# Decode attention with grouped queries on one core: scores with queries in rows, probabilities transposed back, values two chunks at once

## The chip, the cores and the metric

The kernel runs on one core of one Trainium2 chip. Its time is the device time of one execution in microseconds (us), and the median of the runs is quoted. Each kernel was run in three or five rounds beside the kernel before on the same chip, and every profile quoted is of a run that counts as fast: at most 1.5% above the fastest run of the same kernel in its call. Medians are of all runs. A ratio is the mean time of one kernel's fast runs over that of the other's of the same rounds, so it is not quite the ratio of the medians that stand beside it. A profile is taken of one execution; its span is the time from the first to the last instruction, 1.7 to 1.9 us less than the time of that execution in nearly all runs.

## The reference

Eight sequences of four new tokens attend to a cache of 2048 keys and values with 8 K/V heads of 128; each K/V head serves four query heads. All inputs are bf16.

```python
B, Sq, D = 8, 4, 512
Hq, Hkv, Sk, Dh = 32, 8, 2048, 128
q = (x @ wq).reshape(B, Sq, Hq, Dh).transpose(0, 2, 1, 3)
k = jnp.repeat(k_cache, rep, axis=1)          # rep = 4
v = jnp.repeat(v_cache, rep, axis=1)
scores = jnp.einsum("bhqd,bhkd->bhqk", q, k) * Dh ** -0.5
p = softmax(scores)
o = jnp.einsum("bhqk,bhkd->bhqd", p, v)
out = o.transpose(0, 2, 1, 3).reshape(B, Sq, Hq * Dh) @ wo
```

K and V are 67 MB together, the weights 8 MB more. Each byte is used for 16 queries only, so the kernel is a race between loading the cache and touching it once.

## The kernel before

The work is cut into 32 units: a pair of K/V heads of one sequence, with 1 MB of K and 1 MB of V. A unit has 32 chunks of keys, 64 keys of each head in the 128 partitions. K is transposed on TensorE (two bf16 read as one fp32), copied to SBUF, and used as the stationary operand of the scores, with the 32 query columns moving. The exps write probabilities with keys in the partitions, which is the layout in which they then move against V as the stationary operand. The sums of the softmax are a matmul with a matrix of ones. Transposes run 3.5 units ahead of the values.

```python
pad0 = const.tile([128, 192], BF16, name="pad0")     # first of the const tiles
...
ones = const.tile([128, 128], BF16, name="ones")
pad = const.tile([128, 64], BF16, name="pad")        # read and written by nothing
probs = [const.tile([128, C, NQ], BF16, name=f"probs{i}") for i in range(L // 2 + 2)]
...
def scores(i):                                        # a half unit
    for j in range(HC // 2):
        for e in range(2):
            nc.tensor.matmul(s_ps[:, 2*j : 2*j+2, :], lhsT=k_t[:, j % (HC // 4), :, e],
                             rhs=q_bd[:, p, e, b, :, :], start=(e == 0), stop=(e == 1))
    for g in range(2):                                # exp straight into probs
        nc.scalar.activation(out=pr[rows, ..., cols], in_=s_ps[rows, :, cols], func=EXP)

def values(i):
    for c in range(HC):
        nc.tensor.matmul(o_ps[u][:, :], lhsT=vs[u][:, cc, :], rhs=pr[:, cc, :], ...)

def norms(u):                                         # ones x probs, reduce, reciprocal
    ...
def finish(u):                                        # one multiply, o_ps * r_sb -> oT
    ...
for step in range(-L - 1, NH):                        # NH = 64 half units
    ...                                               # transposes, scores, transposes
    if step >= 0:
        if hf == 0:
            norms(u)
        values(step)
        if hf == 1:
            finish(u)
    load_ready(...)                                   # K: 7 buffers, V: 6
...
to_tokens(2)                                          # end: oT -> rows of wo, projection
project(1, 0, 4); to_wo_rows(2); project(1, 4, 4); ...
```

The softmax here doesn't subtract the row's maximum and nothing guards it: scores larger than these inputs give would overflow.

## Time and profile before

| | before |
|---|---|
| median of the runs | 189.3 us at first, 189.4 to 189.8 in later rounds |
| the execution that was profiled first | 192.02 us, span 190.2, mean clock 0.972 |
| bytes moved | 75.97 MB, mean 399 GB/s |
| busy: TensorE / VectorE / ScalarE | 83% / 59% / 45% |
| chain that ended last | DMA 97% |

The chain is read from the end back: for each piece of work, what released it. Where it says DMA for 97%, the time is that of the loads. Busy shares say less; TensorE at 83% is idle whenever it waits for K. The lines themselves stand in the prediction.

### The profile page before, as it was taken

What the parts mean: (1) busy time and instruction counts of PE and PEld (TensorE: products, weight loads), DVE (VectorE), ACT (ScalarE), POOL (GpSimd) and SP (SyncE); (2) the same over time, 40 slices, a digit from 0 to 9 for tenths busy, and PEclk for the clock granted to TensorE, in tenths of its full rate; (3) what the DMA queues carried; (4) which work ended last, traced back from release to release, by engine and by line L of the source; (5) the groups of instructions that cost most, each with busy time, mean ns of one, the idle gap of its engine ahead of it and who ended that gap; (6) DMA issues with size and microseconds to landing.
All of it is one profiled execution on the core that took longest, in us unless ns stands there. A gap on an engine that the chain in (4) does not pass through costs nothing.

```text
span 190.2 us, 6461 instructions
## 1 busy us (share of the span) xinstructions
PE 156.9 (83%) x2899; PEld 139.3 (73%) x2899; DVE 113.0 (59%) x218; ACT 86.4 (45%) x170; POOL 6.3 (3%) x9
## 2 busy tenths in 40 slices
PE   0536596999978888999988999978888889999693
PEld 0516396899967777889977888878877778886471
DVE  0580545577756666757766666665666668676420
ACT  2003656565555555445555555554555554454000
POOL 8400000000000000000000000000000000000000
PEclk9999879999999999999999999999999999999858
DMA  6999999999999999999999999999999999999970
GB/s 245 451 407 382 383 394 394 386 385 387 397 419 426 422 426 424 426 422 427 424 424 426 426 422 431 417 427 422 426 424 427 420 429 420 424 424 415 416 310 22
DMA packets 10955, 75.97 MB, mean 399 GB/s; under 512 B 1288, under 2 KB 1416, under 8 KB 2568
## 3 DMA queue, kind: packets, MB, share of 16 engines
q1 hardware_dynamic: 10880, 75.55, 96.4%
q8 instruction: 22, 0.36, 0.7%
q14 instruction: 5, 0.04, 0.1%
q10 hardware_dynamic: 48, 0.02, 0.0%
HBM read 75.53 MB, written 0.03 MB: 397 GB/s over the span
## 4 chain that ended last, share of the span: by engine, by line
DMA 97%; SPq 1%; issue 0%; PE 0%; ACT 0%
DMA k_sb<-in_k_cache_dram 69%; DMA v_sb<-in_v_cache_dram 8%; DMA wo_e<-in_wo_dram 8%; DMA wq_sb<-in_wq_dram 7%; DMA wo_sb<-in_wo_dram 4%; SPq L131 0%; PE out_ps L376 0%; SPq L111 0%; ACT out_sb L430 0%; SPq L121 0%
## 5 line engine op out<-in xcount | busy, mean ns | idle before, releaser
L195 PE MATMUL kp<-ident,k_sb 128*128 128x128 f32 x512 | 82.7, 288 | 20.5 <-DMA k_sb<-in_k_cache_dram 10.5
L202 DVE COPY kt<-kp 128x1024 bf16<-128x1024 bf16 x96 | 65.5, 686 | 28.3 <-PE kp L195 27.4
L266 ACT ACTIVATE probs<-s_ps 64x256 bf16<-64x256 f32 x128 | 48.5, 379 | 69.9 <-PE s_ps L256 69.1
L195 PEld LDWEIGHTS kp<-ident,k_sb 128*128 128x128 f32 x512 | 55.8, 144 | 23.9 <-DMA k_sb<-in_k_cache_dram 12.5
L256 PE MATMUL s_ps<-q_bd,kt 128*128 128x64 bf16 x1024 | 42.5, 195 | 3.1 <-ACT kt L200 1.9
L256 PEld LDWEIGHTS <-kt 128*128 128x128 bf16 x1024 | 40.0, 99 | 5.5 <-ACT kt L200 2.2
L280 PEld LDWEIGHTS <-v_sb 128*128 128x128 bf16 x1024 | 34.4, 96 | 9.5 <-DMA v_sb<-in_v_cache_dram 2.1
L200 ACT COPY kt<-kp 128x1024 bf16<-128x1024 bf16 x32 | 32.4, 1012 | 12.6 <-PE kp L195 11.8
L280 PE MATMUL o_ps<-probs,v_sb 128*128 128x32 bf16 x1024 | 35.1, 177 | 1.2 <-DMA v_sb<-in_v_cache_dram 1.1
L302 DVE TENSOR_REDUCE l_sb<-l_ps 128x32 f32<-128x512 f32 x32 | 22.1, 692 | 21.2 <-PE l_ps L294 21.2
L294 PE MATMUL l_ps<-probs,ones 128*128 128x512 bf16 x64 | 19.0, 379 | 0.0
L306 DVE RECIPROCAL r_sb<-l_sb 128x32 f32<-128x32 f32 x32 | 11.3, 353 | 1.1
L311 DVE TENSOR_TENSOR oT<-o_ps,r_sb 128x32 bf16<-128x32 f32 x32 | 5.8, 182 | 1.9 <-PE o_ps L280 1.7
L294 PEld LDWEIGHTS <-ones 128*128 128x128 bf16 x64 | 6.1, 98 | 0.5
L430 ACT CAST out_sb<-out_ps 64x256 bf16<-64x256 f32 x1 | 0.4, 366 | 13.1 <-PE out_ps L376 13.1
L376 PE MATMUL out_ps<-wo_sb,oP 128*32 128x256 bf16 x48 | 5.5, 393 | 0.1
L171 POOL MEMSET wo_e<- 64x6144 bf16 x1 | 5.2, 5212 | 0.3 <-POOLq L447 0.3
L243 DVE CAST q_bd<-pse 64x512 bf16<-64x512 f32 x4 | 2.6, 683 | 4.3 <-PE pse L234 4.3
L376 PEld LDWEIGHTS <-oP 128*32 128x32 bf16 x48 | 3.5, 137 | 1.4 <-issue 0.2
L178 DVE COPY pick<-ident 128x64 bf16<-128x64 bf16 x4 | 0.6, 220 | 6.5 <-POOL ident masks.py:199 6.5
L219 PE MATMUL psq<-xT_sb,wq_sb 128*128 128x32 bf16 x128 | 3.5, 186 | 0.3 <-DVE xT_sb L213 0.3
L219 PEld LDWEIGHTS <-wq_sb 128*128 128x128 bf16 x128 | 3.5, 103 | 0.3 <-issue 0.3
(41 smaller groups left out, 31.9 us busy)
## 6 DMA issues: line engine op xcount, KB each, us to landing
k_sb<-in_k_cache_dram SPq DMA_DIRECT2D x32, 1024.0 KB, 19.6
v_sb<-in_v_cache_dram SPq DMA_DIRECT2D x32, 1024.0 KB, 19.4
wq_sb<-in_wq_dram SPq DMA_DIRECT2D x1, 4096.0 KB, 14.1
wo_sb<-in_wo_dram SPq DMA_DIRECT2D x4, 512.0 KB, 14.8
wo_sb<-in_wo_dram SPq DMA_DIRECT2D x4, 256.0 KB, 9.6
wo_m<-in_wo_dram SPq DMA_DIRECT2D x1, 512.0 KB
wo_e<-in_wo_dram SPq DMA_DIRECT2D x8, 60.0 KB
x_sb<-in_x_dram SPq DMA_DIRECT2D x1, 32.0 KB
```

What stands on the lines that cost most here:

```text
L195: nc.tensor.transpose(kp[:, j, :], k4[:, w : w + 128], ident4[:, :])
L200: nc.scalar.copy(out=kt2, in_=kp2)
L202: nc.vector.tensor_copy(out=kt2, in_=kp2)
L219: nc.tensor.matmul(psq[:, h, :], lhsT=wq_sb[:, r, hh * 128 : (hh + 1) * 128], rhs=xT_sb[:, r, :], start=(r == 0), stop=(r == R - 1),)
L256: nc.tensor.matmul(s_ps[:, 2 * j : 2 * j + 2, :], lhsT=k_t[:, j % (HC // 4), :, e], rhs=q_bd[:, p, e, b, :, :], start=(e == 0), stop=(e == 1),
L266: nc.scalar.activation(out=pr[rows, hf * HC : (hf + 1) * HC, cols], in_=s_ps[rows, :, cols], func=EXP)
L280: nc.tensor.matmul(o_ps[u][:, :], lhsT=vs[u][:, cc, :], rhs=pr[:, cc, :], start=(cc == 0), stop=(cc == C - 1),)
L294: nc.tensor.matmul(l_ps[:, :, :], lhsT=ones[:, :], rhs=pr[:, c : c + LC, :], start=(c == 0), stop=(c + LC == C),)
L302: nc.vector.tensor_reduce(out=l_sb[:, :], in_=l_ps[:, :, :].rearrange("d c q -> d q c"), axis=AX, op=ADD)
L306: nc.vector.reciprocal(r_sb[:, :], l_sb[:, :])
L311: nc.vector.tensor_tensor(out=oT[(p + 1) // 2][:, :, (p == 2) * 1, b, :], in0=o_ps[u][:, :].rearrange("d (h s) -> d h s", h=HP), in1=r_sbs ...
L376: nc.tensor.matmul(out_ps[half * T : (half + 1) * T, :], lhsT=o, rhs=w[:, half * DH : (half + 1) * DH], start=(p == 0 and r == 0), stop=(p ...
```

## The change

The intent is to take work off TensorE and ScalarE. The scores use the small query matrix as the stationary operand (32 columns, four column tiles at once) and move K past it with 256 columns, so a unit needs 16 pairs of weight load and matmul instead of 32. The exps then have queries in the partitions, so ScalarE sums for the softmax as it goes; the probabilities are transposed back on TensorE and copied. The values use the probabilities as the stationary operand (64 columns, two column tiles) and move two chunks of V at once. That leaves sums and outputs spread over partitions, and two small fp32 matmuls each ("norms" and "finish") fold them per unit. Both write to `psum_l`, a pool with a single bank (a bank is a part of PSUM, the memory that matmuls write their results to).

```diff
-    psum_s = ctx.enter_context(tc.tile_pool(name="psum_s", bufs=2, ...))
+    psum_s = ctx.enter_context(tc.tile_pool(name="psum_s", bufs=1, ...))
+    psum_t = ctx.enter_context(tc.tile_pool(name="psum_t", bufs=1, ...))
...
-    ones = const.tile([128, 128], BF16, name="ones")
+    fold = const.tile([128, 2, NQ], FP32, name="fold")
+    spread = const.tile([128, 2, 4, 2, HQ], FP32, name="spread")
+    by_q = const.tile([128, HQ], FP32, name="by_q")
     pad = const.tile([128, 64], BF16, name="pad")
-    probs = [const.tile([128, C, NQ], BF16, ...) for i in range(L // 2 + 2)]
+    probs = [const.tile([128, J, 2, 2, HQ], BF16, ...) for i in range(3)]
...
+    def scores(u):
+        for g in range(2):
+            for e in range(2):
+                for t in range(4):
+                    nc.tensor.matmul(s_ps[t * 32 : (t + 1) * 32, :, g, :],
+                        lhsT=q_bd[:, p, e, b, g, :, :],
+                        rhs=kt[(u, t)][:, :, g * 64 : (g + 1) * 64, e], ...)
+        for g in range(2):
+            nc.scalar.activation(out=s_sb[:, :, g, :], in_=s_ps[:, :, g, :], func=EXP,
+                                 accum_out=l_sb[:, g : g + 1])
+    def probs_to_keys(u):                 # 4 transposes, 2 copies on ScalarE
+    def norms(u):                         # 2 fp32 matmuls into psum_l, reciprocal
+    def values(u):
+        o_ps = psum_o.tile([128, 2 * Dh], FP32, tag="o", name="o_ps")
+        for i in range(J):                # 16, alternating PSUM rows 0:64 and 64:128
+            nc.tensor.matmul(o_ps[a : a + 64, :], lhsT=pr[:, i, ...], rhs=vs[u][:, c : c + 2, :], ...)
+        nc.scalar.mul(out=o_sb, in_=o_ps[:, :], mul=r_sbs[u][:, 0:1])
     def finish(u):
+        f_ps = psum_l.tile([128, NQ], FP32, tag="l", name="f_ps")
+        for c in range(2):
+            nc.tensor.matmul(f_ps[:, :], lhsT=o_sbs[u][:, c, :], rhs=fold[:, c, :], ...)
+        nc.vector.tensor_copy(out=oT[...], in_=f_ps[:, :])
...
+    for n in range(NU + A):               # A = 3
+        w = n - A
+        transposes 0, 1 of unit n
+        if w >= 1:
+            finish(w - 1)
+        probs_to_keys(n - 2); scores(n - 1)
+        transposes 2, 3 of unit n
+        if w >= 0:
+            norms(w)
+            values(w)
+        load_ready(...)
+    finish(NU - 1)
     to_tokens(2)
```

More of the change, by code (lines that the diff above doesn't have):

```diff
@@ L36 @@
     NQ = 2 * rep * Sq
-    HC = C // 2
+    HQ = rep * Sq
+    J = C // 2
+    JT = J // 4
     HP = 2 * rep
@@ L40 @@
     NU = G2 * B
-    NH = 2 * NU
     KB = 7
     VB = 6
-    L = 6
-    KA = L // 2 + 1
+    A = 3
+    KA = A + 1
     WR = HP
@@ L52 @@
     AX = mybir.AxisListType.X
-    LC = 16
     ADD = mybir.AluOpType.add
@@ L63 @@
     psum_k = ctx.enter_context(tc.tile_pool(name="psum_k", bufs=3, space=bass.MemoryType.PSUM))
-    psum_s = ctx.enter_context(tc.tile_pool(name="psum_s", bufs=2, space=bass.MemoryType.PSUM))
+    psum_s = ctx.enter_context(tc.tile_pool(name="psum_s", bufs=1, space=bass.MemoryType.PSUM))
+    psum_t = ctx.enter_context(tc.tile_pool(name="psum_t", bufs=1, space=bass.MemoryType.PSUM))
     psum_o = ctx.enter_context(tc.tile_pool(name="psum_o", bufs=1, space=bass.MemoryType.PSUM))
@@ L80 @@
     qT_all = const.tile([128, G2, B, HP, Sq], BF16, name="qT_all")
-    q_bd = const.tile([128, G2, 2, B, 2, NQ], BF16, name="q_bd")
+    q_bd = const.tile([128, G2, 2, B, 2, 2, HQ], BF16, name="q_bd")
     pick = const.tile([128, 2, 2, Dh // 2], BF16, name="pick")
@@ L97 @@
     ident = const.tile([128, 128], BF16, name="ident")
-    ones = const.tile([128, 128], BF16, name="ones")
+    fold = const.tile([128, 2, NQ], FP32, name="fold")
+    spread = const.tile([128, 2, 4, 2, HQ], FP32, name="spread")
+    by_q = const.tile([128, HQ], FP32, name="by_q")
     pad = const.tile([128, 64], BF16, name="pad")
-    probs = [const.tile([128, C, NQ], BF16, name=f"probs{i}") for i in range(L // 2 + 2)]
+    probs = [const.tile([128, J, 2, 2, HQ], BF16, name=f"probs{i}") for i in range(3)]
     units = [(p, b) for p in range(G2) for b in range(B)]
@@ L180, with transpose_part @@
             )
-    nc.vector.memset(q_bd[:, :, :, :, :, :], 0.0)
-    nc.vector.memset(ones[:, :], 1.0)
+    nc.vector.memset(q_bd[:, :, :, :, :, :, :], 0.0)
     for t in probs:
-        nc.vector.memset(t[:, :, :], 0.0)
+        nc.vector.memset(t[:, :, :, :, :], 0.0)
+    nc.vector.memset(spread[:, :, :, :, :], 0.0)
+    nc.vector.tensor_tensor(
+        out=fold[:, :, :],
+        in0=ident4[:, : 2 * NQ].rearrange("p (c q) -> p c q", c=2),
+        in1=ident4[:, 2 * NQ :].rearrange("p (c q) -> p c q", c=2),
+        op=ADD,
+    )
+    nc.vector.tensor_reduce(
+        out=by_q[:, :], in_=ident4[:, :].rearrange("p (c q) -> p q c", q=HQ), axis=AX, op=ADD
+    )
+    for g in range(2):
+        for c in range(4):
+            nc.vector.tensor_copy(out=spread[:, g, c, g, :], in_=by_q[:, :])
     kt = {}
-    def transpose_part(i, part):
-        u, hf = divmod(i, 2)
-        c0 = hf * HC + part * (HC // 2)
-        kp = psum_k.tile([128, HC // 4, 128], FP32, tag="k", name="kp")
+    def transpose_part(u, t):
+        kp = psum_k.tile([128, JT, 128], FP32, tag="k", name="kp")
         k4 = ks[u][:, :, :].rearrange("s c d -> s (c d)").bitcast(FP32)
-        for j in range(HC // 4):
-            w = (c0 // 2 + j) * 128
+        for j in range(JT):
+            w = (t * JT + j) * 128
             nc.tensor.transpose(kp[:, j, :], k4[:, w : w + 128], ident4[:, :])
-        kp2 = kp[:, :, :].rearrange("k j s -> k (j s)").bitcast(BF16)
-        k_t = ktpool.tile([128, HC // 4, 128, 2], BF16, tag="kt", name="kt")
-        kt2 = k_t[:, :, :, :].rearrange("k j s e -> k (j s e)")
-        if part == 1 and hf == 1:
-            nc.scalar.copy(out=kt2, in_=kp2)
-        else:
-            nc.vector.tensor_copy(out=kt2, in_=kp2)
-        kt[(i, part)] = k_t
-    for i in range(2):
-        for part in range(2):
-            transpose_part(i, part)
+        k_t = ktpool.tile([128, JT, 128, 2], BF16, tag="kt", name="kt")
+        nc.vector.tensor_copy(
+            out=k_t[:, :, :, :].rearrange("k j s e -> k (j s e)"),
+            in_=kp[:, :, :].rearrange("k j s -> k (j s)").bitcast(BF16),
+        )
+        kt[(u, t)] = k_t
+    for t in range(4):
+        transpose_part(0, t)
     xtp = psum_o.tile([128, R, T], BF16, tag="o", name="xtp")
@@ L214 @@
     for p in range(G2):
-        psq = psum_s.tile([128, HP, T], FP32, tag="s", name="psq")
+        psq = (psum_t.tile([128, HP, T], FP32, tag="t", name="psq")
+               if p % 2 else psum_s.tile([128, HP, T], FP32, tag="s", name="psq"))
         for h in range(HP):
@@ L232 @@
         for e in range(2):
-            pse = psum_s.tile([128, 2, B, NQ], FP32, tag="s", name="pse")
+            pse = (psum_t.tile([128, 2, B, 2, HQ], FP32, tag="t", name="pse")
+                   if e else psum_s.tile([128, 2, B, 2, HQ], FP32, tag="s", name="pse"))
             nc.tensor.matmul(
-                pse[:, :, :, :],
+                pse[:, :, :, :, :],
                 lhsT=pick[:, e, :, :],
@@ L243 @@
                 (nc.scalar.copy if g else nc.vector.tensor_copy)(
-                    out=q_bd[rows, pp : pp + 2, e, :, g, :], in_=pse[rows, :, :, :]
+                    out=q_bd[rows, pp : pp + 2, e, :, :, g, :].rearrange("d p b g q -> d p (b g) q"),
+                    in_=pse[rows, :, :, :, :].rearrange("d p b g q -> d p (b g) q"),
                 )
     wo_sb = wpool.tile([128, G2 - 1, WR, D], BF16, tag="w", name="wo_sb")
-    def scores(i):
-        u, hf = divmod(i, 2)
+    s_sbs = {}
@@ L250, in scores @@
+    l_sbs = {}
+    def scores(u):
         p, b = units[u]
-        pr = probs[u % len(probs)]
-        s_ps = psum_s.tile([128, HC, NQ], FP32, tag="s", name="s_ps")
-        for j in range(HC // 2):
-            k_t = kt[(i, j // (HC // 4))]
-            for e in range(2):
-                nc.tensor.matmul(
-                    s_ps[:, 2 * j : 2 * j + 2, :],
-                    lhsT=k_t[:, j % (HC // 4), :, e],
-                    rhs=q_bd[:, p, e, b, :, :],
-                    start=(e == 0),
-                    stop=(e == 1),
-                )
+        s_ps = psum_s.tile([128, JT, 2, 64], FP32, tag="s", name="s_ps")
+        for g in range(2):
+            for e in range(2):
+                for t in range(4):
+                    nc.tensor.matmul(
+                        s_ps[t * 32 : (t + 1) * 32, :, g, :],
+                        lhsT=q_bd[:, p, e, b, g, :, :],
+                        rhs=kt[(u, t)][:, :, g * 64 : (g + 1) * 64, e],
+                        start=(e == 0),
+                        stop=(e == 1),
+                    )
+        s_sb = small.tile([128, JT, 2, 64], BF16, tag="s_sb", name="s_sb")
+        l_sb = small.tile([128, 2], FP32, tag="l_sb", name="l_sb", bufs=A + 1)
+        for g in range(2):
+            nc.scalar.activation(
+                out=s_sb[:, :, g, :], in_=s_ps[:, :, g, :], func=EXP, accum_out=l_sb[:, g : g + 1]
+            )
+        s_sbs[u], l_sbs[u] = s_sb, l_sb
@@ L263, in scores @@
+    def probs_to_keys(u):
+        pt = psum_t.tile([128, JT, 128], BF16, tag="t", name="pt")
+        for j in range(JT):
+            nc.tensor.transpose(
+                pt[:, j, :], s_sbs[u][:, j, :, :].rearrange("q g s -> q (g s)"), ident[:, :]
+            )
+        pr = probs[u % len(probs)]
         for g in range(2):
             rows = slice(g * 64, (g + 1) * 64)
-            cols = slice(g * NQ // 2, (g + 1) * NQ // 2)
-            nc.scalar.activation(
-                out=pr[rows, hf * HC : (hf + 1) * HC, cols], in_=s_ps[rows, :, cols], func=EXP
-            )
@@ L270 @@
-    o_ps = {}
-    def values(i):
-        u, hf = divmod(i, 2)
-        p, b = units[u]
-        pr = probs[u % len(probs)]
-        if hf == 0:
-            o_ps[u] = psum_o.tile([128, NQ], FP32, tag="o", name="o_ps")
-        for c in range(HC):
-            cc = hf * HC + c
-            nc.tensor.matmul(
-                o_ps[u][:, :],
-                lhsT=vs[u][:, cc, :],
-                rhs=pr[:, cc, :],
-                start=(cc == 0),
-                stop=(cc == C - 1),
+            nc.scalar.copy(
+                out=pr[rows, :, :, g, :].rearrange("s j c q -> s (j c) q"),
+                in_=pt[rows, :, :].rearrange("s j (c q) -> s (j c) q", q=HQ),
@@ L290, in norms @@
     def norms(u):
-        pr = probs[u % len(probs)]
-        l_ps = psum_l.tile([128, LC, NQ], FP32, tag="l", name="l_ps")
-        for c in range(0, C, LC):
-            nc.tensor.matmul(
-                l_ps[:, :, :],
-                lhsT=ones[:, :],
-                rhs=pr[:, c : c + LC, :],
-                start=(c == 0),
-                stop=(c + LC == C),
-            )
-        l_sb = small.tile([128, NQ], FP32, tag="l_sb", name="l_sb")
-        nc.vector.tensor_reduce(
-            out=l_sb[:, :], in_=l_ps[:, :, :].rearrange("d c q -> d q c"), axis=AX, op=ADD
-        )
@@ L305, in norms @@
-        r_sb = small.tile([128, NQ], FP32, tag="r_sb", name="r_sb")
-        nc.vector.reciprocal(r_sb[:, :], l_sb[:, :])
-        r_sbs[u] = r_sb
+        l_ps = psum_l.tile([128, 1], FP32, tag="l", name="l_ps")
+        for g in range(2):
+            nc.tensor.matmul(
+                l_ps[:, :],
+                lhsT=spread[:, g, :, :, :].rearrange("k c g q -> k (c g q)"),
+                rhs=l_sbs[u][:, g : g + 1],
+                start=(g == 0),
+                stop=(g == 1),
+            )
@@ new lines, in norms @@
+        r_sb = small.tile([128, 1], FP32, tag="r_sb", name="r_sb")
+        nc.vector.reciprocal(r_sb[:, :], l_ps[:, :])
+        r_sbs[u] = r_sb
+    o_sbs = {}
+    def values(u):
+        pr = probs[u % len(probs)]
+        o_ps = psum_o.tile([128, 2 * Dh], FP32, tag="o", name="o_ps")
+        for i in range(J):
+            j, t = divmod(i, 4)
+            c = 2 * (t * JT + j)
+            a = i % 2 * 64
+            nc.tensor.matmul(
+                o_ps[a : a + 64, :],
+                lhsT=pr[:, i, :, :, :].rearrange("s c g q -> s (c g q)"),
+                rhs=vs[u][:, c : c + 2, :].rearrange("s c d -> s (c d)"),
+                start=(i < 2),
+                stop=(i >= J - 2),
+            )
+        o_sb = small.tile([128, 2, Dh], FP32, tag="o_sb", name="o_sb")
+        nc.scalar.mul(
+            out=o_sb[:, :, :].rearrange("q c d -> q (c d)"), in_=o_ps[:, :], mul=r_sbs[u][:, 0:1]
+        )
+        o_sbs[u] = o_sb
@@ L309, in finish @@
     def finish(u):
         p, b = units[u]
-        nc.vector.tensor_tensor(
+        f_ps = psum_l.tile([128, NQ], FP32, tag="l", name="f_ps")
+        for c in range(2):
+            nc.tensor.matmul(
+                f_ps[:, :],
+                lhsT=o_sbs[u][:, c, :],
+                rhs=fold[:, c, :],
+                start=(c == 0),
+                stop=(c == 1),
+            )
+        nc.vector.tensor_copy(
             out=oT[(p + 1) // 2][:, :, (p == 2) * 1, b, :],
-            in0=o_ps[u][:, :].rearrange("d (h s) -> d h s", h=HP),
-            in1=r_sbs[u][:, :].rearrange("d (h s) -> d h s", h=HP),
-            op=mybir.AluOpType.mult,
+            in_=f_ps[:, :].rearrange("d (h s) -> d h s", h=HP),
@@ L382, in project @@
                 )
-    for step in range(-L - 1, NH):
-        i, j = step + L + 1, step + L
-        if 1 < i < NH:
-            transpose_part(i, 0)
-        if 0 <= j < NH:
-            scores(j)
-        if 1 < i < NH:
-            transpose_part(i, 1)
-        u, hf = divmod(step, 2)
-        if step >= 0:
-            p, b = units[u]
-            if hf == 0:
-                norms(u)
-            values(step)
-            if hf == 1:
-                finish(u)
-            elif p in (1, 3) and b == 1:
+    for n in range(NU + A):
+        w = n - A
+        for t in range(2):
+            if 0 < n < NU:
+                transpose_part(n, t)
+        if w >= 1:
+            finish(w - 1)
+        if 0 <= n - 2 < NU:
+            probs_to_keys(n - 2)
+        if 0 <= n - 1 < NU:
+            scores(n - 1)
+        for t in range(2, 4):
+            if 0 < n < NU:
+                transpose_part(n, t)
+        if w >= 0:
+            p, b = units[w]
+            norms(w)
+            if p in (1, 3) and b == 1:
                 to_tokens(p // 2)
-            elif p in (1, 3) and b == 2:
+            values(w)
+            if p in (1, 3) and b == 2:
                 to_wo_rows(p // 2)
-        load_ready(min((i + 1) // 2, NU), max((step + 1) // 2, 0))
-        if step == NH - 1 - 2 * VB:
+        load_ready(min(n + 1, NU), max(w + 1, 0))
+        if w == NU - 1 - VB:
             assert not loads
@@ L412 @@
                 load_wo(3, r, 2)
-        if step == 28:
+        if w == 13:
             out_ps = psum_e.tile([2 * T, DH], FP32, tag="e", name="out_ps")
-        if 28 <= step < 36 and step % 2:
-            project(0, (step - 29) // 2 * 3, 3)
-        if step == NH - 3:
+        if 14 <= w < 18:
+            project(0, (w - 14) * 3, 3)
+        if w == NU - 2:
             project(0, WE, WM + 1)
+    finish(NU - 1)
     to_tokens(2)
```

## The prediction

> **What bounds the kernel now.** I read first the page's slices and its chain of work that ended last, then the waits of the queue that issues the DMAs (SP), then the timeline of one unit in the steady middle, and last the timeline of the end. Part 2 and part 4 of the page:
>
> ```profile
> DMA  6999999999999999999999999999999999999970
> GB/s 245 451 407 382 383 394 394 386 385 387 397 419 426 422 426 424 426 422 427 424 424 426 426 422 431 417 427 422 426 424 427 420 429 420 424 424 415 416 310 22
> ...
> DMA 97%; SPq 1%; issue 0%; PE 0%; ACT 0%
> ```
>
> The DMA engines are busy in every slice but the first and the last two, and the chain is 97% DMA. The kernel moves 75.97 MB; nothing in the change touches one of these bytes. The two levels of the rate (about 388 GB/s until slice 10, about 424 after) are not TensorE's doing either: the three windows of 4 us from 12 to 24 us, where TensorE is busy 1.43, 3.76 and 2.08 us, already have the low rate (380 to 394); it ends about when the last of the small wo_e loads, issued at 36 us, have landed. So is a load ever held back by a buffer that compute frees late? The waits of the DMA queue over the whole span:
>
> ```profile
> SPq L121 <- DMA v_sb<-in_v_cache_dram: 47.0, 22, 3.0
> SPq L111 <- DMA k_sb<-in_k_cache_dram: 46.5, 22, 2.9
> ...
> SPq L111 <- PE kp L195: 0.7, 2, 0.4
> ...
> SPq L121 <- PE kp L195: 0.5, 2, 0.3
> ```
>
> The queue waits for earlier loads to land (columns: us in total, times, longest), and for a compute engine to free a buffer only 1.2 us in all. In the built program an issue waits for the load eight before it. At 19.6 us from issue to landing (part 6) eight loads of 1 MB are always in flight, and 13 K and V buffers stand behind them.
>
> How near is TensorE? K loads are issued at 83.82, 88.75, 93.63, 98.58 us: 4.9 us for a unit (one K and one V load). The weight loads of a unit that did not wait, from the timeline:
>
> ```profile
> 92.40 0.42 PEld L195 LDWEIGHTS kp<-ident,k_sb 128*128 128x128 f32 x4
> 92.79 0.21 PEld L294 LDWEIGHTS <-ones 128*128 128x128 bf16 x2
> 93.12 0.67 PEld L280 LDWEIGHTS <-v_sb 128*128 128x128 bf16 x16
> 93.71 0.42 PEld L195 LDWEIGHTS kp<-ident,k_sb 128*128 128x128 f32 x4
> 94.10 0.68 PEld L256 LDWEIGHTS <-kt 128*128 128x128 bf16 x16
> 94.71 0.42 PEld L195 LDWEIGHTS kp<-ident,k_sb 128*128 128x128 f32 x4
> 95.10 0.56 PEld L280 LDWEIGHTS <-v_sb 128*128 128x128 bf16 x16
> 95.59 0.42 PEld L195 LDWEIGHTS kp<-ident,k_sb 128*128 128x128 f32 x4
> 95.97 0.61 PEld L256 LDWEIGHTS <-kt 128*128 128x128 bf16 x16
> ...
> 96.91 0.21 PEld L294 LDWEIGHTS <-ones 128*128 128x128 bf16 x2
> ```
>
> From norms to norms (L294) TensorE takes 4.12 us, by start-to-start: four groups of transposes 1.56, two of scores 1.16, two of values 1.08, norms 0.33. It then waits for K. So it has 0.8 us of slack per unit; the 83% "busy" of the page says less than that, as ends are modelled and overlap.
>
> The end is the one stretch where compute shows:
>
> ```profile
> 179.24 0.91 PEld L280 LDWEIGHTS <-v_sb 128*128 128x128 bf16 x32 [1.55 <-DMA v_sb<-in_v_cache_dram]
> ...
> 180.29 0.19 DVE L311 TENSOR_TENSOR oT<-o_ps,r_sb 128x32 bf16<-128x32 f32 x1 [1.00 <-PE o_ps L280]
> ...
> 182.97 3.59 PEld L376 LDWEIGHTS <-oP 128*32 128x32 bf16 x37
> ...
> 186.79 0.11 PEld L376 LDWEIGHTS <-oP 128*32 128x32 bf16 x3 [0.23 <-issue]
> 187.22 0.37 ACT L430 CAST out_sb<-out_ps 64x256 bf16<-64x256 f32 x1 [13.10 <-PE out_ps L376]
> ```
>
> The last V tile lands at 179.2; values, normalising, transposes and the last projection follow, while the wo_sb loads land, the last at 186.75. The projection (182.97 to 187.19) had caught up with them to within 0.23 us: the chain names the DMA, but TensorE's path from the last V ends at the same time. It runs slow there: the windows 180 to 186 us show a granted clock of 0.50.
>
> **What the Trainium skill says.** "TensorEngine Tiling (Array Packing)", Key Properties: tiles run matmuls in parallel, and changing the tiling mode drains TensorE. The trace agrees on both: six 256-column matmuls of out_ps on wo_e (two column tiles) at 105.38 lasted 0.50 us, the last one 0.27 of it, so one started each 46 ns; and the weight load after them stood 0.21 us on "issue". The same page, Restrictions: column tiling disables the fast weight load; here, 32-column weights loaded at (0.22-0.09)/5 = 26 ns each, so I take 52 ns for 64 columns. "FP8 and Floating Point Precision", TensorE Precision Notes: true fp32 takes four passes. No run here shows it yet; L195 is fp32 but a transpose (98 ns each). "TensorE: Matmul & The Clock Gate", Part 1: an idle TensorE drops to half clock and needs about 3.4 us of activity to come back; the 0.50 above agrees.
>
> **The change part by part,** per unit. Counting the built programs, TensorE pairs (weight load and matmul) fall from 2899 to 2195. Outside the units both have 2899-32x82 = 275; so the new unit has (2195-275)/32 = 60: 16 K transposes, 16 scores, 4 transposes back, 16 values, and 8 for four fp32 matmuls, two pairs each.
>
> - Transposes of K: unchanged, 1.56 us.
> - Scores: 32 pairs at 1.16 us become 16 with 256 moving columns in four column tiles. At the 46 ns seen with two tiles, 0.74 us; with four nearer the pair rate of values (0.49/16 = 30 ns), 0.48. I take 0.6.
> - Transposes back: four bf16 pairs, estimated 0.06 each (half of the fp32 ones' 0.098, and a little), 0.25 us.
> - Values: 32 pairs at 1.08 us become 16 in two column tiles, at 52 ns 0.85 us.
> - Two exits from column tiling at 0.21: 0.4 us.
> - Norms 0.33 us go; eight fp32 pairs come. At the 0.098 of an fp32 transpose 0.8 us; at double 1.6. I take 1.0.
>
> Sum: 1.56+0.6+0.25+0.85+0.4+1.0 = 4.65 us, more than today's 4.12 in spite of fewer instructions, but below 4.9. DVE: four kt copies at 0.686 (one comes from ScalarE), reciprocal and folded copy some 0.2 each: 3.1 us against 3.3. ScalarE: exps two at about 0.38 (it was four) plus two reads of sums estimated 0.2, two copies 0.38, one scaling 0.38: 2.3 us against 2.5. Each wait within an iteration spans other work: transposes back take the exps of the iteration before, and folding lies behind eight transposes (0.78 us) that cover the scaling. So in the middle all of it lies beside the loads and is worth nothing. Fewer instructions to fetch (0.36 MB in the queue of instructions, perhaps a quarter less) return some 0.2 us.
>
> The end pays. Now from the last V to the first transpose of oT: 179.24 to 180.54, 1.3 us. Then: sixteen values, about four before the clock drops and twelve at 0.105 (the 40 projections of 256 columns took 4.22 us at half clock), with the last one's latency 1.8 us; scaling on ScalarE 0.45; four fp32 pairs at half clock, 0.185 each as the transposes at 23.8 us had, plus latency, 1.0; copy 0.25. Sum 3.5: 2.2 us later. Of this 0.2 is absorbed by the wait before the last projections, and some half microsecond may come back as TensorE's clock returns before the delayed projections are done. Net about +1.5, less the 0.2: +1.3 us.
>
> **Rivals.** (1) TensorE becomes the bound. By my estimate the first two, shorter iterations end at about 28 us (scores start at 23.05 today, L256), 29 full ones follow, three partial ones (7 us) and the end (8 us): 43+29P for a period P. This passes today's span of 190 only at P of about 5.1, and 2% more at 5.2. For it: fp32 pairs at double, scores that do not overlap in four tiles, more drains (P to 5.7, then 208 us). Against: the 46 ns measured for two tiles and the margin of catching up. I give it one in eight. (2) Nothing at the end: the clock stays up because the longer values keep TensorE active, or the wo loads cover the delay: 189.1. For it: the projections warm up at about 186 in the old trace; against: the slack measured there is 0.23 us. (3) A faster kernel: compute is hidden and the bytes are the same, so more than 0.5 us is hard to find; 2% would need 3.8 us less DMA time. (4) A buffer held longer starves a load: K and V buffers stay 7 and 6 with the same lookahead of 3 units, and from the order of loads I estimate that a buffer comes free 5 us or more before the load that reuses it is issued; no effect.
>
> **Range and chances.** 189.3 + 1.3 = 190.6 us. The low side is rival 2 with its margin, 188.8; the high side a fully cold, longer end or a slightly binding TensorE, 193.0. Faster by over 2% 0.01, slower 0.12, the rest within.
>
> **What would show it.** The DMA row still full and the chain mostly DMA; the last V landing within 0.5 us of 179.2; K transposes waiting for K loads in the middle, so P under 4.9; a first oT transpose (L324's successor) about 2 us later after the last V, with scaling and fp32 folding in between; the projections then ending the chain on TensorE rather than DMA. I am wrong if the queue waits for TensorE or the rate in the middle falls below 420 GB/s (rival 1), or if the end is no longer than before (rival 2).

## The result, and the profile after

The changed kernel took 195.67 us (193.65 to 196.27 in 4 runs) against 189.51; the ratio is 1.031 (95% interval 1.023 to 1.038). It is slower by 3%, where 0.7% was forecast, and outside the range. The profile of after is of an execution of 196.04 us, span 194.3.

The page of after, parts 2 and 4 (busy tenths of the DMA engines and their rate in 40 slices; the chain by engine):

```profile
DMA  5999999999999999999999999999999999999700
GB/s 213 435 432 422 414 429 418 419 414 423 418 413 420 423 418 420 422 418 422 413 422 415 420 418 422 415 422 418 420 418 417 417 420 422 416 416 400 294 22 7
...
DMA 83%; PE 10%; issue 3%; ACT 1%; POOL 0%; SPq 0%; DVE 0%; POOLq 0%
```

The DMA engines are as full as before until the 37th slice, and then TensorE ends alone: a tenth of the chain is now its work. Two things can be read against the page of before. The rate has no low stretch at the start, and from the fourth slice to the 36th it stays between 413 and 429, where before it was mostly 420 to 430 in the middle. And the last two slices, some 10 us, load nearly nothing.

Did TensorE hold up the loads? The waits of the DMA queue in after (us in total, times, longest):

```profile
SPq L126 <- DMA v_sb<-in_v_cache_dram: 48.0, 22, 3.1
SPq L116 <- DMA k_sb<-in_k_cache_dram: 47.5, 22, 3.0
...
SPq L126 <- PE kp L210: 4.5, 12, 0.4
```

Hardly: 4.5 us in twelve short waits, none over 0.4 us, while eight loads are under way. And a unit on TensorE, from the timeline of after (start, duration, engine, line, operation, tiles, shapes):

```profile
96.45 0.53 PEld L307 LDWEIGHTS l_ps<-l_sb,spread 128*128 128x128 f32 x4
96.99 0.80 PEld L329 LDWEIGHTS <-probs 128*64 128x64 bf16 x16
98.02 0.86 PEld L210 LDWEIGHTS kp<-ident,k_sb 128*128 128x128 f32 x8 [0.24 <-DMA k_sb<-in_k_cache_dram]
98.85 0.53 PEld L346 LDWEIGHTS f_ps<-fold,o_sb 128*128 128x128 f32 x4
99.21 0.32 PEld L291 LDWEIGHTS <-s_sb 128*128 128x128 bf16 x4
99.64 0.35 PEld L273 LDWEIGHTS <-q_bd 128*32 128x32 bf16 x16
100.20 0.86 PEld L210 LDWEIGHTS kp<-ident,k_sb 128*128 128x128 f32 x8 [0.22 <-issue]
101.03 0.53 PEld L307 LDWEIGHTS l_ps<-l_sb,spread 128*128 128x128 f32 x4
```

From norms to norms it is 4.58 us, against 4.12 before. The wait of 0.24 put down to K is mostly the exit from column tiling, which takes 0.22 at 100.20, where no load is waited for, and 0.20 behind the next unit's values. What shows that loads set the pace is that K transposes start 0.02 to 0.03 us after the queue's next K issues (98.00 and 102.98), each of which waits for an earlier K to land: 4.98 us from load to load. So the middle is bound by loads, as predicted, though with little to spare: the second of these units, with six projections in it, leaves no wait beyond the exit. The end is not. The last pieces of the chain of after, in order of time (start, duration, what):

```profile
178.82 0.99 PE o_ps L329 x16
...
180.57 0.57 PE f_ps L346 x4
181.14 0.02 issue
181.17 0.20 DVE oT L353
181.37 0.04 issue
181.41 0.61 PE l_ps L307 x4
182.02 1.01 PE o_ps L329 x16
183.03 0.03 issue
183.06 0.48 ACT o_sb L337
...
184.71 0.82 PE nat L364 x6
...
187.20 4.03 PE out_ps L416 x40
```

The reader is to see a relay: values of unit 30 (178.82), some projections, folding of unit 30 (180.57), its copy on VectorE, only then the norms of unit 31 (181.41), then its values (182.02), scaling, folding, and the tail. No load stands in it. In the prediction values of unit 31 started when their V landed. The projections between (0.76 us) stand ahead of the folding in TensorE's order as well; by the end of the scaling (180.32) it could have started up to 0.2 us sooner without them.

### The profile page after: what moved, and what is told of

It reads as the page before. It is cut to its first block, busy times and chain, and to the rows that moved or that the text cites.

```text
span 194.3 us, 5244 instructions
## 1 busy us (share of the span) xinstructions
PE 167.6 (86%) x2195; PEld 142.7 (73%) x2195; DVE 99.8 (51%) x226; ACT 84.5 (44%) x234; POOL 6.3 (3%) x9
## 4 chain that ended last, share of the span: by engine, by line
DMA 83%; PE 10%; issue 3%; ACT 1%; POOL 0%; SPq 0%; DVE 0%; POOLq 0%
DMA k_sb<-in_k_cache_dram 61%; DMA wo_e<-in_wo_dram 13%; DMA v_sb<-in_v_cache_dram 9%; PE out_ps L416 3%; PE o_ps L329 2%; PE f_ps L346 2%; PE kp L210 1%; PE l_ps L307 1%; ACT o_sb L337 1%; PE s_ps L273 1%; PE nat L364 0%; PE perm L386 0%; DVE oT L353 0%; PE pt L291 0%; SPq L116 0%
## 5 line engine op out<-in xcount | busy, mean ns | idle before, releaser
L212 DVE COPY kt<-kp 128x1024 bf16<-128x1024 bf16 x128 | 82.2, 686 | 57.7 <-PE kp L210 57.5
L210 PEld LDWEIGHTS kp<-ident,k_sb 128*128 128x128 f32 x512 | 56.1, 143 | 30.9 <-DMA k_sb<-in_k_cache_dram 11.7
L297 ACT COPY probs<-pt 64x512 bf16<-64x512 bf16 x64 | 37.1, 579 | 47.8 <-PE pt L291 47.5
L329 PE MATMUL o_ps<-v_sb,probs 128*64 128x256 bf16 x512 | 34.2, 276 | 0.0
L329 PEld LDWEIGHTS <-probs 128*64 128x64 bf16 x512 | 25.6, 109 | 0.5
L283 ACT ACTIVATE s_sb<-s_ps 128x256 bf16<-128x256 f32 x64 | 23.9, 379 | 0.5 <-PE s_ps L273 0.2
L273 PE MATMUL s_ps<-kt,q_bd 128*32 128x256 bf16 x512 | 20.4, 278 | 0.0
L346 PE MATMUL f_ps<-fold,o_sb 128*128 128x32 f32 x128 | 17.6, 261 | 1.7 <-ACT o_sb L337 1.7
L346 PEld LDWEIGHTS f_ps<-fold,o_sb 128*128 128x128 f32 x128 | 17.0, 193 | 2.6 <-ACT o_sb L337 2.5
L307 PEld LDWEIGHTS l_ps<-l_sb,spread 128*128 128x128 f32 x128 | 16.8, 191 | 0.9 <-DVE oT L353 0.6
L307 PE MATMUL l_ps<-l_sb,spread 128*128 128x1 f32 x128 | 16.4, 232 | 0.3 <-DVE oT L353 0.3
```

Source lines behind the costliest of these rows:

```text
L210: nc.tensor.transpose(kp[:, j, :], k4[:, w : w + 128], ident4[:, :])
L212: nc.vector.tensor_copy(out=k_t[:, :, :, :].rearrange("k j s e -> k (j s e)"), in_=kp[:, :, :].rearrange("k j s -> k (j s)").bitcast(BF16),)
L273: nc.tensor.matmul(s_ps[t * 32 : (t + 1) * 32, :, g, :], lhsT=q_bd[:, p, e, b, g, :, :], rhs=kt[(u, t)][:, :, g * 64 : (g + 1) * 64, e], s ...
L283: nc.scalar.activation(out=s_sb[:, :, g, :], in_=s_ps[:, :, g, :], func=EXP, accum_out=l_sb[:, g : g + 1])
L297: nc.scalar.copy(out=pr[rows, :, :, g, :].rearrange("s j c q -> s (j c) q"), in_=pt[rows, :, :].rearrange("s j (c q) -> s (j c) q", q=HQ),)
L307: nc.tensor.matmul(l_ps[:, :], lhsT=spread[:, g, :, :, :].rearrange("k c g q -> k (c g q)"), rhs=l_sbs[u][:, g : g + 1], start=(g == 0), s ...
```

## The experiments

Twelve kernels were run, all with correct results. The first four asked what belongs to the end and what to the middle.

**before_again.** No edit.

> The kernel before, unchanged, to have more of its runs with their span and granted clock: the profile of before took 192.0 us, 2.3 more than the median of the runs. If the clock at the end decides (theory C), its runs split by mean clock: near 189.5 us with a clock of about 1.0, near 192 with 0.97. If the rate of the early loads decides (rival D: the profile of before moved 388 GB/s until 50 us, that of after 418), the profile of a run near 189.5 shows the higher early rate and perhaps the same low clock at the end.

Measured: 189.5 us (14 runs, 189.14 to 192.49). This time an execution of 189.21 us was profiled, span 187.4. Its chain at the end, and its window from 24 to 150 us (busy us of each engine with counts, then granted clock, DMA share, GB/s):

```profile
160.37 16.02 DMA v_sb<-in_v_cache_dram
...
176.40 7.54 DMA wo_sb<-in_wo_dram
...
183.98 0.41 PE out_ps L376 x4
```

```profile
24.00:150.00 126.00, 116.94 (x2165) 108.08 (x2187) 83.42 (x160) 68.66 (x138) 0.00 (x0) 0.99 1.01 424
```

The first profile had misled me twice. It had 388 GB/s until 50 us; this one has 424 and 426 in the windows 36 to 50 and 24 to 36, with the same small loads of wo_e under way, so these loads are not what makes that rate low. And TensorE's clock is 1.00 from 176 to 184 us here, where the first profile had 0.50 from 180 to 186: the projections finish early and wait for each piece of wo_sb. The last V lands at 176.4 us instead of 179.2. The runs of before do fall in two groups: of 48, 36 lie between 189.06 and 190.68 us and 12 between 191.57 and 193.46. Theory C, a split by mean clock, failed: runs of 192.42 and 192.49 us had 0.981 and 0.987, one of 189.72 had 0.954. Rival D fits better. Of the profiles whose loads lie on a 512-byte or 256-byte grid (see below), two have a low early rate (24 to 50 us: 389 GB/s in the first profile of before, 401 in that of vf_al512_bf16_warm, 424 to 426 in the others), and both are of executions some 2 to 3 us above the median of their kernel. That is two executions, so it is not shown for the group. A cold end (TensorE at half clock) costs this kernel little: in the profile of before_off256, a kernel as fast as before, the clock is 0.50 from 180 us on, and from the landing of the last V to the end of the last copy it takes 8.5 us, against 8.4 here.

**after_again.** No edit.

> The changed kernel, unchanged. Theory T (the drain of the last three units is a serial chain of about 3.2 us a unit and ends about 4 us later than before): about 195.5 us, and again values of the last unit starting about 2 us after its V has landed. By C its runs spread from 193.5 (clock 1.0) to 196.3 (clock 0.965).

Measured: 195.19 us (193.8 to 196.07), ratio 1.029. Its window against that of before_again:

```profile
24.00:150.00 126.00, 119.91 (x1570) 103.53 (x1563) 73.11 (x160) 62.94 (x181) 0.00 (x0) 1.00 1.01 419
```

The DMA share is the same, 1.01, and the rate 419 instead of 424 GB/s. It was 419 in every profile of the unaligned changed kernels. From 6 to 12 us both have 437 GB/s. The window 12 to 24 does not separate the kernels yet: 415 to 421 in the profiles with shifted loads, 417 to 422 in the others that have no low early rate.

**values_first.** In the last three iterations there is no K left to transpose, so the values of a unit can come ahead of the folding of the unit before, if they have a bank of their own:

```diff
+        if u >= NU - A:
+            o_ps = psum_k.tile([128, 2 * Dh], FP32, tag="k", name="o_ps")
-        if w >= 1:
+        if 1 <= w and n < NU:
             finish(w - 1)
...
             values(w)
+            if n >= NU:
+                finish(w - 1)
```

> The changed kernel, but in the last three iterations (no K left to transpose) the values of a unit come before the folding of the unit before, with their PSUM tiles in the banks that the K transposes no longer use. Theory T: values of the last unit start when its V lands, about 180 instead of 182.0 us, and the time falls by about 2 us against after_again (to about 193.5). Rival M (the middle lost it: 4.97 us a unit in the profile of after against 4.89): no change, within 0.5 us.

Measured: 192.91 us (192.77 to 194.39), ratio 1.019: 2.3 us faster than after_again. Its chain at the end:

```profile
163.69 16.38 DMA v_sb<-in_v_cache_dram
...
180.09 7.63 DMA wo_sb<-in_wo_dram
...
187.75 0.41 PE out_ps L419 x4
```

The last V lands at 180.07 and its values start at 180.11 (in after, with the load issued at the same 163.65, they started at 182.02). The end is bound by loads again, as in before. So the relay of the drain cost about 2.3 us (1.9 by the means of the runs). But this kernel is still 3 us slower than before, and its chain names only loads: the last V lands 3.7 us later than in before_again. Rival M's forecast of no change failed, but the middle did lose time too, at the rate of the loads; whether TensorE has a part in that is tested below.

**own_bank.** Only the folding of the last four units gets banks of its own, so norms need not wait for VectorE to empty the fold before:

```diff
+        if u >= NU - A - 1:
+            f_ps = psum_k.tile([128, NQ], FP32, tag="k", name="f_ps")
```

> The changed kernel, but the last four units fold into PSUM banks of the K transposes, so that norms no longer wait for the copy of the fold before. If that single buffer is what holds the drain: about 1.2 us faster than after_again (three times 0.4). If the wait of the fold for the scaling on ScalarE holds it, which stays: less than 0.7 us.

Measured: 193.74 us (192.87 to 195.22), ratio 1.022: 1.5 us faster than after_again. In its chain the values of unit 31 follow with no VectorE between:

```profile
180.19 0.56 PE f_ps L349 x4
180.75 0.42 PE l_ps L307 x4
181.17 1.01 PE o_ps L329 x16
```

They start 0.85 us earlier than in after (0.1 of it is earlier loads). Two waits of 0.4 us went, not three; the medians differ by somewhat more than that, but the ranges overlap, so the step from 0.85 to 1.5 is not explained by this profile. The single PSUM bank shared by sums and folds is thus some 0.75 us of the 2.1 by which these values followed their V. That the order makes up the rest is inferred from values_first; the two repairs were not tried together.

**Where the rate went.** The loads are the same in number, size and order. What differs in them is where they go: the compiled programs place the first K tile at byte 98304 of each partition in before and at 95296 in after. The first is a multiple of 512 (of 8192 even), the second 64 over one. The `pad` tile, which nothing uses, had the size that brings this about (probably on purpose; the code does not say), and the new constants (`fold`, `spread` and `by_q` are 1344 bytes where `ones` was 256; two probs tiles fewer are 4096) moved everything behind it off that grid. (The first loads, wq and four K tiles, go to shifted places too, and yet the rate of 6 to 12 us is the same; why, no run shows.)

**after_al512.** The pad alone is grown:

```diff
-    pad = const.tile([128, 64], BF16, name="pad")
+    pad = const.tile([128, 288], BF16, name="pad")
```

> The changed kernel with its unused pad tile grown from 128 to 576 bytes per partition, so that the K and V tiles start on a multiple of 512 bytes again (in before the first starts at 98304, in after at 95296, which is 64 over a multiple of 512). Theory A (the shift of the load targets costs DMA rate, 419 against 424 GB/s, from 12 us on): the rate returns to about 424 and the last V lands about 2.5 us sooner; the time falls from 195.2 to about 193. Rival E (the engines' new accesses to SBUF slow the loads): 419 GB/s and 195.2 us as after_again.

Measured: 193.02 us (192.11 to 193.59), ratio 1.017: 2.2 us faster than after_again. That one ran on another chip, but the ratio to before fell by as much (1.029 to 1.017), and the last V is issued at 161.31 instead of 163.56 us. Its window:

```profile
24.00:150.00 126.00, 121.68 (x1591) 105.46 (x1589) 74.43 (x162) 64.26 (x184) 0.00 (x0) 1.00 1.01 425
```

The rate is 425 GB/s with all the new accesses of the engines, so rival E falls.

**before_off64.** The reverse: the kernel before, with its pad 64 bytes larger and nothing else changed.

> The kernel before with its unused pad tile grown by 64 bytes per partition, so that K and V tiles lie 64 bytes over a multiple of 512, with nothing else changed. Theory A: the rate of the middle falls to about 419 GB/s and the time rises by 2 to 3.5 us, to about 192. Rival E: 189.5 us and 424 GB/s as before.

Measured: 191.85 us (191.7 to 191.88), ratio 1.012 (1.009 to 1.014): 2.1 to 2.3 us slower than before, at 418 GB/s, with the last V issued at 162.59 instead of 160.37 us:

```profile
24.00:150.00 126.00, 116.89 (x2147) 106.82 (x2145) 82.29 (x158) 67.17 (x134) 0.00 (x0) 0.96 1.01 418
```

Some 2.2 us taken out of one kernel and put into the other by one unused tile is as clean as such a test gets. It also settles whether the queue's waits for TensorE made the rate low (rival 4 of the prediction): they are 1.9 us in all here, against 5.7 in after, and the rate is as low.

**before_off192 and before_off256.** What is the grid, and does the offset matter? The Trainium skill ("DMA: Bandwidth & Descriptors", How a descriptor splits into AXI transactions) gives 256 bytes as the grain, and says that the bytes below an unaligned start are moved for nothing. The pad is 192 and 256 bytes larger.

> The kernel before with its pad grown by 192 bytes, so K and V tiles lie 192 bytes over a multiple of 256. The Trainium skill (DMA: Bandwidth & Descriptors, How a descriptor splits into AXI transactions) says that a transfer must start at a multiple of 256 bytes and that the bytes below its start are moved for nothing: 6 beats of 32 bytes on 256 for each 8 KB row, against 2 at 64. By this the rate falls further, to about 415 GB/s or below, and the time is 1 to 3 us above before_off64 (191.85). If any start off the grain costs one extra piece of the same size: as before_off64, 418 GB/s and 191.9 us.

> The kernel before with its pad grown by 256 bytes: K and V tiles on a multiple of 256 but not of 512. If the grain is 256, as that page says: 424 GB/s and 189.5 us. If it is 512: about 418 GB/s and 192 us.

Measured: 191.9 us (191.78 to 192.22, ratio 1.012) for 192, and 189.61 us (ratio 1.001, interval 0.999 to 1.004) for 256. Their windows:

```profile
24.00:150.00 126.00, 113.22 (x2118) 104.40 (x2141) 82.77 (x158) 67.08 (x134) 0.00 (x0) 0.99 1.01 418
```

```profile
24.00:150.00 126.00, 117.01 (x2164) 108.29 (x2186) 83.36 (x160) 68.50 (x138) 0.00 (x0) 0.99 1.01 424
```

Of the offsets tried, 256 costs nothing, as the page has it, and 64 and 192 cost the same 1.4% of the rate (1.2% of the time). The expectation from the page's count of beats for 192 (a further fall) failed; the other branch, one extra piece of the same size for any start off the grain, fits.

**vf_al512.** Both repairs, values first and the larger pad.

> values_first (192.9 us) with the tiles aligned as in after_al512. If the late drain and the shifted tiles are the whole loss and add up: 190.0 us, within 1 us of before, with the last loads of wo_sb ending the chain. If something else slows the loads (rival E): 192.9 as values_first.

Measured: 191.22 us (17 runs, 189.99 to 196.91), ratio 1.0075 (1.005 to 1.010). After_again was 5.4 us above the median of before in its call, this is 1.5 above, and 1.2 more than expected. The two repairs add up: by the means of the fast runs, each against before, values first saved 1.9 us, the pad 2.1, and both together 4.0. So the rest is a third thing. Its chain:

```profile
140.61 20.52 DMA k_sb<-in_k_cache_dram
...
161.20 16.65 DMA v_sb<-in_v_cache_dram
...
177.89 1.06 PE o_ps L332 x16
...
180.78 0.82 PE nat L367 x6
```

The last K but one is issued when it was in before_again (140.61 against 140.70) but takes 20.5 us to land instead of 19.6, and the last V, whose issue waits for it, lands 1.5 us later. From there to the first transpose of oT it takes 2.9 us, against 1.3; yet to the end of the last copy it is 8.5 us, against 8.4, so this longer path cost nothing here.

The queues of the two profiles show where the first 0.9 us arise: three V issues in a row, first in vf_al512, then in before_again.

```profile
148.01 6.22 SPq L126 DMA_DIRECT2D v_sb<-in_v_cache_dram  x3
148.10 5.25 SPq L121 DMA_DIRECT2D v_sb<-in_v_cache_dram  x3
```

Most K and V issues of the middle are 2.3 to 2.6 us apart, but now and then an earlier load lands some 0.9 us late and the next issue comes after 3.3 to 3.5 us. Before_again has two such steps after 40 us (at 54.2 and 123.7), as has before_off256; vf_al512 has three (40.9, 96.7 and 153.9), and so has every version of the changed kernel. The third is the one above. What makes a step is not known.

**vf_al512_bf16.** As vf_al512, with `fold` and `o_sb` in bf16, which halves the pairs of a fold (the pad is 352 columns wide, to keep the same place).

> vf_al512 with o_sb and the folding matrix in bf16 instead of fp32, so two pairs instead of four for a fold. By the theory that loads bound the middle: the unit's period without waits falls by about 0.25 us, hidden; the end is a few tenths shorter at most. 189.7 us, not faster than before by more than 0.5 us. If TensorE were the bound: about 5 us faster.

Measured: 191.1 us (190.01 to 194.55), ratio 1.006. The difference of 0.1 us to vf_al512 says nothing; above all it is not 5 us, so TensorE isn't the bound.

**after_warm.** The changed kernel with idle matmuls of 512 columns where TensorE waits at the end: one before the last norms, two after the last values, one before and two after the transposes of oT.

```diff
+    def warm(k):
+        w_ps = psum_s.tile([128, 512], FP32, tag="s", name="w_ps")
+        for i in range(k):
+            nc.tensor.matmul(w_ps[:, :], lhsT=ident[:, :], rhs=<512 columns of q_bd>, start=True, stop=True)
```

> The changed kernel with a few idle matmuls of 512 columns (0.21 us each) into a free PSUM bank where TensorE waits in the last microseconds. Theory C (part of the loss is TensorE's clock of one half in the last projections, 4.1 us for 40 instead of about 2): clock about 1.0 at the end and about 193.5 us instead of 195.2, with less spread. If the clock is not what the end waits for: 195.2 or a little more.

Measured: 193.88 us (five of six runs 193.68 to 193.92), 1.3 us faster than after_again, with clock 1.00 from 180 to 190 us and the last projections in 2.31 us instead of 4.03:

```profile
186.65 2.31 PE out_ps L416 x40
```

So 1.3 us of the median loss comes through the clock. The four runs of the result point the same way: mean clocks of 0.965, 0.964, 0.990 and 1.000 go with spans of 194.4, 194.3, 193.5 and 191.9 us. But the mean clock is no measure of the end alone, and the six runs of after_again don't line up like that: 0.973 goes with spans of 192.7, 193.9 and 194.3. This isn't a third share beside the other two: in the profile of values_first, where the relay is gone, the clock stays at 1.00 to 190 us and the projections wait for their loads. It is how a late end becomes longer still.

**vf_al512_bf16_warm.** Idle matmuls in the best version, at the same places but one: four of them stand between the last norms and the last values, instead of one before those norms.

> vf_al512_bf16 (191.1 us, median) with the same idle matmuls. If its rest over before (1.5 us) is the clock at the end: 189.0 to 189.6 us, level with before or up to 0.5 us faster. If the rest is a later last V or the longer path behind it: 190.5 or more.

Measured: 190.66 us (22 runs, 189.93 to 194.39), ratio 1.005 (1.003 to 1.008). The clock accounts for little of the rest. The fastest run is 0.9 us above the fastest of before (189.06). The execution profiled was one of 192.59 us, and its window from 24 to 36 us shows the low early rate again:

```profile
24.00:36.00 12.00, 12.00 (x158) 9.79 (x157) 9.00 (x17) 6.81 (x21) 0.00 (x0) 1.00 1.01 388
```

No version beat the kernel before, so none is recommended over it.

## Why the prediction was wrong

**What bounds the kernel.** Right: loads bound the middle before and after, and the queue waits for loads. The period of a unit on TensorE was predicted as 4.65 us and is 4.58, of which 0.24 is the wait behind values. By term, as start-to-start in the timeline: K transposes 1.66 (predicted 1.56), scores with the exit from column tiling 0.56 (0.8), values with theirs 1.03 (1.05), transposes back 0.43 (0.25), the fp32 pairs 0.54+0.36 = 0.90 (1.0). ScalarE's copies were under-sized, 0.58 instead of 0.38, without effect. So rival 1, to which a chance was given, was rightly set aside. "Slower", to which 0.12 was given, came true for other reasons.

**The step that failed first: "nothing in the change touches one of these bytes".** It does not change their number, but it changes where they are written. I compared instructions and never the addresses of the tiles that loads fill. The "last V landing within 0.5 us of 179.2" and "the rate in the middle falls below 420 GB/s (rival 1)" were named as signs. The last V landed at 179.9, 0.7 off; the rate fell to 419, and the cause was not rival 1. The shift cost 2.2 us (after_al512) or 2.1 to 2.3 us (before_off64).

**The step that failed second: the end.** The prediction counted from the landing of the last V, as if the values of the last unit started then. They started at 182.0 us, 2.1 after it landed (179.9; the last issue of wo_sb waits for that load). In the full iterations eight K transposes (0.83 us) cover the scaling on ScalarE, and the prediction said so; in the last three iterations there are none, each unit's folding waits for scaling, the norms of the next wait for the copy of that fold in the one bank they share, and values wait for norms: 3.2 us from values to values (178.82 to 182.02). I used the pipeline's full iteration for the wait and forgot its drain. From the start of these values to the first transpose of oT it then took 2.7 us, less than the 3.5 summed for it, because the clock fell only after 184 us and not in the middle of the values. Giving values priority returned 2.3 us (1.9 by the means).

**The base.** The prediction added its shift, read from a profile of the 192.0 us execution, to the median of the runs. How the profiles differ shows best when each is cut at the landing of the last V (us; the tail is from there to the end of the last copy, out_sb; the clock is that of TensorE from 180 to 186 us):

| profile | last V lands | tail | clock |
|---|---|---|---|
| before, shown in the prediction | 179.2 | 8.4 | 0.50 |
| before_again | 176.4 | 8.4 | 0.95 |
| after | 179.9 | 11.7 | 0.82 |
| after_warm | 179.9 | 9.5 | 1.00 |
| values_first | 180.1 | 8.5 | 1.00 |
| after_al512 | 177.4 | 11.7 | 0.63 |
| vf_al512 | 177.9 | 8.5 | 0.72 |

The two profiles of before have the same tail at either clock. What the slow execution hid is the landing: against it the last V of after is only 0.7 us late, against before_again it is 3.5, and this with 3.3 of a longer tail makes up the 6.9 us between the spans of 187.4 and 194.3. The prediction had 0 and 1.3 for the two. The loads moved off the grid are 2.5 of the 3.5 (after_al512). Rival 2 hoped for a warm end in after; the profiles of after and after_again lost it (1.3 us by after_warm in the medians).

**The first reading of the rate was wrong too.** The low rate until slice 10 was put down to the wo_e loads; before_again has the same loads and 424 to 426 GB/s.

**What stays open.** After both repairs 1.5 us remain between vf_al512 and before. In the profiles it is the landing of the last V, 1.5 us later at an unchanged rate: it is issued 0.8 us later, after the third step in the landings, and takes 0.6 us longer itself (16.65 against 16.02), which need not come from the change, as before_off256 has it too (16.64). Why the changed kernel has three steps and before two was not found. The path behind the last V didn't count in that profile, but it can: vf_al512_bf16 has a tail of 9.3 us, with a clock of 0.50 from 180 to 184. With idle matmuls and bf16 folding 1.3 us still remain in the median. Nor was it found what makes the early loads slow in a part of the runs of either kernel.

## What to carry to other kernels

When a kernel is bound by loads, compare the addresses of their targets before and after a change, not only the instructions: a few constants more moved every K and V tile 64 bytes off the grid and cost 1.2%, and a tile that nothing uses may be there for that. Work out the drain of a software pipeline separately from its full iteration, with the waits that the missing work no longer covers and the buffers that are single. And before adding a shift to a median, check that the profile it was read from is of a typical run.

## What the Trainium skill lacked or had wrong

- "DMA: Bandwidth & Descriptors", How a descriptor splits into AXI transactions: the 256-byte grain was right for the SBUF side of these loads (offset 256: 424 GB/s; 64: 418), but the cost did not follow the wasted beats. By its count 64 bytes waste 2 of 256 beats (an estimate of 0.8%) and 192 bytes 6 (2.3%); both measured 418 against 424 GB/s, 1.4%, as if any start off the grain cost the same. That page's rules for kernel authors do not say to place load targets on that grain.
- "TensorEngine Tiling (Array Packing)", Key Properties: it says that a change of tiling mode drains TensorE but not for how long. Here 0.20 to 0.22 us stood on "issue" at an exit where no load was waited for. Four column tiles of 256 columns started a matmul each 24 ns ((0.64-0.28)/15), against 46 ns with two.
- "FP8 and Floating Point Precision", TensorE Precision Notes: four passes for true fp32. The program has two pairs of weight load and matmul for one fp32 matmul, and four pairs took 0.36 us (32 columns) and 0.54 us (one column, up to the next weight load), so some 0.18 to 0.27 us for a small one; no page that was consulted gives such a figure. How many passes a pair makes, no run shows.
- No page that was consulted tells that one program may load at 390 GB/s from 24 to 36 us in one execution and at 426 in another (the two profiles of before), or what causes it.
